# Three Strassen blocks in place of two, the first begun with four weight slices in the plain way

## The chip, the cores and the metric

One core of one Trainium2 chip runs the program. Its engines are TensorE (PE, matmul; PEld its weight loads), VectorE (DVE), ScalarE (ACT), GpSimd (POOL) and SyncE (SP, which here issues nearly all DMAs). They work side by side, each in the order of its own program, and wait for each other by semaphores. The metric is the time of one execution on the device in microseconds; lower is better. The kernel before takes 587.42 us in the median of three runs (587.04 to 587.86).

## The reference

Windowed attention over 4 x 8 heads, then a two-layer network over all 3072 tokens:

```python
for c in range(nc):                       # chunks of 32 queries
    k_full = concat([mem_k, k[l_start:r_end]])      # 8 memory keys, 16 left, 32 own, 8 right
    scores = scale * q_c @ k_full.T
    a = exp(scores - max); a = a / (sum(a) + 1e-09)
    out[c] = a @ v_full
x = out as (3072 tokens, 512)
h = x @ w_in                              # 512 x 2048
g = maximum(h, 0) + alpha * minimum(h, 0)
y = g @ w_out                             # 2048 x 512
```

All is fp32. A product of two fp32 numbers is made on PE as three products of a high and a low part (low x high, high x low, high x high): each operand is split into a rounded part and what is left of it. So every matrix of weights or tokens needs a split (a cast and a subtraction), and every product is three matmuls.

## The kernel before

**Tiles.** The tokens are eight halves of 384. A unit is one half and one pair of heads (32 units; units 4i to 4i + 3 make half i). `w_in` and `w_out` lie on chip as 16 slices f of 128 hidden features; slice f of both has one place in SBUF (`wps[f]`). A *slice* of a half costs 4 x 3 = 12 matmuls of 384 columns up (L764, `h_ps`), a bend (ACT `below` L773, DVE `bend` L776), a split of the result (ACT `high` L782, DVE `low` L786), and 3 x 3 = 9 matmuls of 512 columns down (L794, `o_ps`).

**The plain part.** Halves 0 to 3 (`NPLAIN = 4`) are made slice by slice. `ORDER` lists these 64 *places*: halves 0 and 1 side by side for the first slices, while the weights arrive and are decoded (ACT and DVE, L674 to L703; slice f is needed at the place of (0, f), so all 16 by place 24), then half 1's rest, then halves 2 and 3. The down products of a place run on PE after the up products of the next one.

**Attention.** Units 0 to 7 are made first, in another way. From place 20 on, pairs of units follow at the places in `BEGIN`: scores on PE (L344), maximum on DVE (L367), exponentials on ACT (L378), scaling on POOL (L399), 28 transposes on DVE (L420), and later the values on PE (L445). `split` leaves the result as a high and a low part for a plain half, `copy_raw` as it is for a Strassen half.

**The Strassen part.** Two blocks of 768 tokens (`NBIG = 2`, `big(s)`): two halves of tokens by two slices of weights make a 2 x 2 product with 7 products (6 matmuls each, L1089, `b_ps`) instead of 8. A *pair* i is two slices. The tokens are turned into seven forms (B11, B21, B22 as they are, T1 to T4 sums; POOL L951, split by ACT L937 and DVE or POOL L941), which lie in the places of weight slices no longer needed (`wps[2]` to `wps[8]`). The sums of weights are made once: `put_far(i, place)` (POOL L874, L877, L884; ACT L881; 12 POOL instructions for each of 8 pairs) is started at place `FIRST_SUM = 26` and every `SUM_EVERY = 3` places, and writes them to HBM; `load(f)` brings them back pair by pair into `wps[9]` to `wps[15]`. Each of the seven products goes into the four results by adds (DVE L1109). The first half's slices are bent, split and sent down with the next pair; the second half's wait (`gs`, `plain`) and go down after the last pair (L1059).

**What sets the order.** `Plan` holds every step with its engine, a cost that the author wrote, what it reads and writes, and how much work should still lie behind it (`rest`). `send` puts the steps out by a list schedule over these costs. On each engine the order is then fixed. The `gate` of a place is written by its up products, and `put_far` waits for that of the place before its own.

Of the kernel before, what the change touches and what calls it, by code (L numbers as in the profile page):

```python
# [37 lines left out]
NPLAIN = 4  # L38
# [58 lines left out]
STARTS_LONG = [x + 1 for x in BEGIN if FIRST_LONG - 1 <= x < len(ORDER)] + [len(ORDER)]  # L97

FORMS = ("T2", "B11", "B21", "T1", "T3", "B22", "T4")
FIRST_SUM, SUM_EVERY = 26, 3  # L100
# [3 lines left out]
FIRST_FRONT = 12  # L104
# [82 lines left out]
def body(ctx: ExitStack, tc: tile.TileContext, qvw, kw, whole, heads, w_in, w_out, alpha, out):  # L187
# [312 lines left out]
    def raw_at(k, half):  # L500

        if half == 0 and k < 2:
            return (k, 0, None), ("tmp", k)
        return spot(k, half % 2, 2)

    def plain_at(at_):

        if at_ not in plain:
            k, hl, blk = at_
            if blk is None:  # L510
                plain[at_] = tmp.tile([P, BT], F32, name="plain", tag=f"o{k}")
# [223 lines left out]
    def hidden(blk, f, first_f, last_f):  # L735

        joint = blk == 1 and f < NJOINT
        place = PLACE[blk, f]
        hk, sd, gh, gl = (x + str(place % n)
# [44 lines left out]
        def low():  # L784
            h["gl"] = room("gl", gl)
            nc.vector.tensor_tensor(out=h["gl"], in0=h["g"], in1=h["gh"].bitcast(F32), op=ALU.subtract)  # L786
# [20 lines left out]
        def add_bend():  # L807
# [3 lines left out]
            step(DVE, 0.56, low, reads=[sd, gh], writes=[gl] + new)  # L811
# [27 lines left out]
    def store(blk, o_ps):  # L839
# [12 lines left out]
        for tt in range(NTT):  # L852
            at_ = (None, None, [("tmp", tt)]) if blk == 1 else leave_at(blk == NPLAIN - 1)
# [74 lines left out]
    def forms(s):  # L928
        slow = ("B11", "B21")

        def split(name, ap, key, p):
            x = FORMS.index(name)

            def high():
                if p == 0:
                    xf[x] = wps[2 + x, 0].tile([P, 2, 2, BT], F32R, name="xf", tag="w")
                nc.scalar.copy(out=xf[x][:, 0, p], in_=plain_at(ap))  # L937

            def low():
                eng = nc.gpsimd if name in slow else nc.vector  # L940
                eng.tensor_tensor(out=xf[x][:, 1, p], in0=plain_at(ap), in1=xf[x][:, 0, p].bitcast(F32), op=ALU.subtract)  # L941

            claim = slot_keys(2 + x) + [("slot", x)] + [("X", x, hl, n) for hl in range(2) for n in range(2)]
            step(ACT, 0.53, high, reads=[key] + ([("slot", x)] if p else []), writes=[("X", x, 0, p)] if p else claim)
            step(*((POOL, 1.05) if name in slow else (DVE, 0.57)), low, reads=[key, ("slot", x), ("X", x, 0, p)], writes=[("X", x, 1, p)])

        for p in range(2):
            (b11, b12), (b21, b22) = [[raw_at(k, 2 * s + h) for h in range(2)] for k in (p, p + 2)]

            def less(to, a, b):  # L950
                step(POOL, 0.95, lambda: nc.gpsimd.tensor_tensor(out=plain_at(to[0]), in0=plain_at(a[0]), in1=plain_at(b[0]), op=ALU.subtract),  # L951
                     reads=[a[1], b[1]], writes=[to[1]])

            split("B11", *b11, p)
            split("B21", *b21, p)
# [29 lines left out]
    def load(f):  # L985
# [19 lines left out]
    def big(s):  # L1005
        ups, downs = UP[s % 2], UP[1 - s % 2]
        half = NPLAIN + 2 * s
        o = [{}, {}]

# [40 lines left out]
        def chunk(which, f, tt, last=NF - 1):  # L1050
            bank = (downs, ups)[which][tt]
            h = g[which, f]

            def go():
                if f == 0:
                    o[which][tt] = bank_of(bank)
                w = wa[s, which, f // 2]
                for i, (gk, wk) in enumerate((("gl", 0), ("gh", 1), ("gh", 0))):
# [3 lines left out]
                        rhs=w[:, f % 2, wk].bitcast(F32R),  # L1062
                        start=(f == 0 and i == 0), stop=(f == NF - 1 and i == 2),
                    )

            pe(0.69, go, [("wa", home[s, which, f // 2]), f"gh{f % 4}", f"gl{f % 4}"], [bank[2]])

        def used(which, i):
            load(home[s, which, i])

        def pair(i):
            n = s * NFP + i
# [3 lines left out]
            def w(x, at_):  # L1076
                return lambda wk, p: wa[n, x][:, at_ + wk * HALF + p * P:at_ + wk * HALF + (p + 1) * P]

            def wide(at_):
                return lambda wk, p: wa[n, 0][:, at_ + wk * 2 * HALF + p * P:at_ + wk * 2 * HALF + (p + 1) * P]  # L1080

            def product(bank, x, weight, name):
# [13 lines left out]
                pe(1.05, go, [("wa", home[n, x])] + [("X", xi, hl, p) for hl in range(2) for p in range(2)], [bank[2]])  # L1096
# [65 lines left out]
            for x in range(2):  # L1162
                load(home[n, x])
# [29 lines left out]
        def meet(olds, news):  # L1193
            attend(0, olds, news, at_=len(ORDER) + clock[0] / PAIR)
            clock[0] += 1.2 + (1.1 if news else 0)
            for u in olds:
                split(u, bank(u)[2])
                if u + 2 < NU:
                    load_v(u + 2)
            for u in news:  # L1200
                unit_begins(u)

        if s == 0:
            for f in queues:
                load(f)
        forms(s)
        news = []
        for i in range(NFP):
            for u in news:
# [177 lines left out]
```

## Time and profile before

| what | value |
|---|---|
| median of 3 runs | 587.42 us (587.04 to 587.86) |
| the profiled execution's own time | 587.05 us |
| its span, first to last instruction | 585.2 us |
| granted clock of PE | 1.00 in every stretch |
| first scores of the second kind (place 20) | 107.88 us |
| begin of POOL's weight sums | 121.2 us |
| begin of the first Strassen block's products | 322.1 us |
| begin of the second one's | 457.0 us |

Times in the profile are microseconds from the first instruction. In a group of instructions stand its line, engine, operation, `out<-in` and count, then its busy time and the mean length of one in ns, then the idle time of the engine just before them and what ended it. Lengths of one engine's instructions may overlap by some 0.05 to 0.1 us, as the next one starts before the last has written all.

### The profile page before, as it was taken

How to read it: one execution, taken by the hardware profiler on the slowest of the kernel's cores; microseconds unless marked ns; L12 is line 12 of the kernel's file. 1: busy time of each engine (PE TensorE's matmuls, PEld its weight loads, DVE VectorE, ACT ScalarE, POOL GpSimd, SP SyncE). 2: the span in 40 equal slices, each digit the busy share in tenths (PEclk: the TensorE clock that was granted, in tenths of full speed). 3: DMA queues.
4: the chain of work that ended last, by engine and by line, in shares of the span. 5: the costliest groups of instructions: out<-in, count | busy, mean ns of one | idle time of the engine just before them, and what ended most of it. 6: DMA issues, size and time to landing. Idle time of an engine off the chain costs nothing.

```text
span 585.2 us, 11938 instructions
## 1 busy us (share of the span) xinstructions
PE 575.6 (98%) x4503; PEld 511.4 (87%) x4503; DVE 435.6 (74%) x965; ACT 294.1 (50%) x774; POOL 145.4 (25%) x194
## 2 busy tenths in 40 slices
PE   7999999999999999999999999999999999999997
PEld 4899999889988989889988999999888999999886
DVE  7979999885948678687598896887959766656420
ACT  3888888725534536546437336336454432323421
POOL 5640000050876383723115000003014100000000
PEclk9999999999999999999999999999999999999999
DMA  8999300226767868551366977777796856776921
GB/s 316 402 416 416 128 0 2 67 66 227 294 231 285 304 204 344 175 192 37 103 200 219 347 255 267 268 286 297 287 297 227 274 231 244 251 285 229 317 92 54
DMA packets 40648, 133.70 MB, mean 228 GB/s; under 512 B 4624, under 2 KB 10000, under 8 KB 34448
## 3 DMA queue, kind: packets, MB, share of 16 engines
q1 hardware_dynamic: 40448, 132.82, 62.9%
q8 instruction: 35, 0.57, 0.4%
q14 instruction: 21, 0.17, 0.1%
q10 hardware_dynamic: 144, 0.13, 0.1%
HBM read 103.57 MB, written 29.36 MB: 227 GB/s over the span
## 4 chain that ended last, share of the span: by engine, by line
PE 87%; POOL 6%; DMA 3%; DVE 2%; issue 1%; ACT 1%; SPq 1%; POOLq 0%
PE b_ps L1059 23%; PE b_ps L1089 20%; PE o_ps L794 18%; PE h_ps L764 18%; PE a_ps L445 3%; PE s_ps L344 2%; POOL sum L874 2%; POOL form L884 2%; POOL sum L877 2%; PE a_ps L610 1%; DMA early<-heads 1%; DMA far_b<-w 1%; PE o_ps L597 1%; DMA qk<-kw 1%; DVE xf L941 1%
## 5 line engine op out<-in xcount | busy, mean ns | idle before, releaser
L764 PE MATMUL h_ps<-xh,w 128*128 128x384 f32 x512 | 130.5, 335 | 0.0
L1089 PE MATMUL b_ps<-xf,wa 128*128 128x384 f32 x672 | 125.3, 335 | 0.1
L1089 PEld LDWEIGHTS b_ps<-xf,wa 128*128 128x128 f32 x672 | 118.1, 188 | 4.8 <-DVE u L1109 0.4
L420 DVE STREAM_TRANSPOSE pt<-e 32x192 f32<-32x192 f32 (+1 forms) x336 | 100.0, 301 | 11.8 <-POOL e L399 6.1
L764 PEld LDWEIGHTS h_ps<-xh,w 128*128 128x128 f32 x512 | 92.7, 188 | 1.1
L764 PE MATMUL h_ps<-xl,w 128*128 128x384 f32 x256 | 87.8, 343 | 0.7 <-DVE g L776 0.6
L794 PE MATMUL o_ps<-w,xh 128*128 128x512 f32 x264 | 82.3, 393 | 0.0
L1109 DVE TENSOR_TENSOR u<-b_ps,u 128x384 f32<-128x384 f32 x112 | 60.2, 554 | 29.5 <-PE b_ps L1089 25.9
L399 POOL TENSOR_TENSOR e<-e,den 128x384 f32<-128x384 f32 x24 | 21.5, 900 | 243.2 <-DVE den L396 123.6
L1024 ACT ACTIVATE g<-u 128x384 f32<-128x384 f32 x64 | 33.5, 525 | 81.7 <-DVE u L1109 77.9
L1059 PE MATMUL b_ps<-wo,xh 128*128 128x512 f32 x192 | 59.8, 393 | 0.0
L1059 PE MATMUL b_ps<-wo,gh 128*128 128x512 f32 x192 | 59.6, 392 | 0.0
L794 PEld LDWEIGHTS o_ps<-w,xh 128*128 128x128 f32 x264 | 49.5, 188 | 9.8
L794 PE MATMUL o_ps<-w,xl 128*128 128x512 f32 x132 | 51.8, 393 | 0.2 <-DVE xl L786 0.2
L764 PEld LDWEIGHTS h_ps<-xl,w 128*128 128x128 f32 x256 | 48.1, 188 | 4.2 <-DVE g L776 1.0
L773 ACT ACTIVATE g<-h_ps 128x384 f32<-128x384 f32 x64 | 31.5, 492 | 40.2 <-PE h_ps L764 38.9
L776 DVE SCALAR_TENSOR_TENSOR g<-g,rise,h_ps 128x384 f32<-128x384 f32 x64 | 39.1, 611 | 16.2 <-ACT g L773 15.2
L378 ACT ACTIVATE e<-s_ps,mx 128x64 f32<-128x64 f32 x144 | 43.3, 318 | 9.9 <-DVE mx L370 9.8
L1059 PEld LDWEIGHTS b_ps<-wo,gh 128*128 128x128 f32 x192 | 36.0, 188 | 6.9
L1059 PEld LDWEIGHTS b_ps<-wo,xh 128*128 128x128 f32 x192 | 36.0, 188 | 6.7
L1059 PE MATMUL b_ps<-wo,xl 128*128 128x512 f32 x96 | 37.6, 391 | 0.0
L1059 PE MATMUL b_ps<-wo,gl 128*128 128x512 f32 x96 | 37.5, 390 | 0.0
(98 smaller groups left out, 874.2 us busy)
## 6 DMA issues: line engine op xcount, KB each, us to landing
wo<-far_o SPq DMA_DIRECT2D x32, 1024.0 KB, 5.1
wa<-far_a SPq DMA_DIRECT2D x16, 1024.0 KB, 4.8
wa<-far_b SPq DMA_DIRECT2D x16, 768.0 KB, 6.2
w_t<-w_in SPq DMA_DIRECT2D x16, 512.0 KB, 9.8
w_t<-w_out SPq DMA_DIRECT2D x16, 512.0 KB, 9.5
far_o<-w SPq DMA_DIRECT2D x16, 512.0 KB, 6.4
qk<-kw SPq DMA_DIRECT2D x24, 272.0 KB, 4.8
v_t<-qvw SPq DMA_DIRECT2D x24, 256.0 KB, 4.9
```

The source lines that it names most:

```text
L378: nc.scalar.activation(out=st["e"][:, i], in_=st["s"][h2][:, n], func=AF.Exp, scale=SCALE, bias=d["mx"][:, u - us[0], n, h2:h2 + 1], accum ...
L399: nc.gpsimd.tensor_tensor(out=st["e"], in0=st["e"], in1=st["den"].broadcast_to([P, NJ * 2, KW]), op=ALU.mult)
L420: nc.vector.transpose(out=pts[u % NPT][quad * CH:(quad + 1) * CH, j, t0:t0 + n1 - n0].rearrange("p t h q -> p (t h) q"), in_=(st["e"], zer ...
L445: nc.tensor.matmul(out=st["a"][h2 * D:(h2 + 1) * D, t * TQ:(t + 1) * TQ], lhsT=st["v"][:, t, h2, :], rhs=pts[u % NPT][:, :, t, h2, :], sta ...
L764: nc.tensor.matmul(out=h["ps"][:, :BT], lhsT=ws[f, 0][:, wk, k * P:(k + 1) * P], rhs=parts(blk, k)[1](xk), start=(k == 0 and n == 0), stop ...
L773: nc.scalar.activation(out=h["g"], in_=h["ps"][:, :BT], func=AF.Relu, scale=-1.0)
L776: nc.vector.scalar_tensor_tensor(out=h["g"], in0=h["g"], scalar=rise[:, f:f + 1], in1=h["ps"][:, :BT], op0=ALU.mult, op1=ALU.add)
L794: nc.tensor.matmul(out=o_ps[tt], lhsT=h[gk][:, tt * P:(tt + 1) * P], rhs=ws[f, 1][:, wk], start=(f == first_f and i == 0), stop=(f == last ...
L1024: nc.scalar.activation(out=h[name], in_=src(), func=AF.Relu, scale=-1.0)
L1059: nc.tensor.matmul(out=o[which][tt], lhsT=h[gk][:, tt * P:(tt + 1) * P], rhs=w[:, f % 2, wk].bitcast(F32R), start=(f == 0 and i == 0), sto ...
L1089: nc.tensor.matmul(out=h[bank[1]][:, :BT], lhsT=weight(wk, p).bitcast(F32R), rhs=xf[xi][:, xk, p], start=p == 0 and k == 0, stop=p == 1 an ...
L1109: nc.vector.tensor_tensor(out=h[t], in0=h[bank[1]][:, :BT], in1=h[t if of is None else of], op=ALU.add)
```

## The change

`NPLAIN` goes from 4 to 2, so that `NBIG` becomes 3: `ORDER` has 32 places, halves 2 and 3 join the Strassen part. Since all weight sums must be in HBM earlier, `put_far` starts at place 9 and not at 26. The first Strassen block does slices 12 to 15 (`BEFORE`) in the plain way, from the weights still on chip, with the tokens' forms B11 and B21 (first half) and then B12 and B22 (second half, a new form that shares its place with T4); the other six pairs are Strassen's. So this block begins before units 14 and 15 have their values. From place 20 on the subtraction `low` goes to POOL, as do those of T3 and T4. The scores and values of units 16 to 31 now fall into blocks 0 and 1, at `AT_PAIR` and `AT_REST`.

```diff
-NPLAIN = 4
+NPLAIN = 2
...
-PAIR, BIG = 4.7, 288.0
-BEGIN = (20, 26, 31, 36, 41, 46, 51, 55, 59, 71.3, 79.1, 86.5)
-AT_PAIR = {3: 26, 6: 28}
-AT_REST = {2: 30, 11: 32}
+PAIR, BIG = 4.7, 438.4
+BEGIN = (20, 24, 28, 32, 36, 40.3, 48.2, 55.8, 59.8, 69.4, 77.3, 85)
+AT_PAIR = ({2: 18, 5: 20}, {3: 26, 6: 28}, {})
+AT_REST = ({2: 22, 11: 24}, {2: 30, 11: 32}, {})
+BEFORE = (12, 13, 14, 15)
...
-FORMS = ("T2", "B11", "B21", "T1", "T3", "B22", "T4")
-FIRST_SUM, SUM_EVERY = 26, 3
+FORMS = ("T2", "B11", "B21", "T1", "T3", "B22", "T4", "B12")
+FIRST_SUM, SUM_EVERY = 9, 3
+FIRST_SLOW = 20
...
+        slow = place >= FIRST_SLOW
...
-            nc.vector.tensor_tensor(out=h["gl"], in0=h["g"], in1=h["gh"].bitcast(F32), op=ALU.subtract)
+            (nc.gpsimd if slow else nc.vector).tensor_tensor(out=h["gl"], in0=h["g"], in1=h["gh"].bitcast(F32), op=ALU.subtract)
...
-            step(DVE, 0.56, low, reads=[sd, gh], writes=[gl] + new)
+            step(*((POOL, 1.05) if slow else (DVE, 0.56)), low, reads=[sd, gh], writes=[gl] + new)
...
-        slow = ("B11", "B21")
+        slow = ("B11", "B21", "T3", "T4")
...
+    pairs_of = [list(range(NFP - len(BEFORE) // 2 if b == 0 else NFP)) for b in range(NBIG)]
...
+        def plain_up(f, which, n):
+            bank = ups[n % 2]
+            names = (("B11", "B21"), ("B12", "B22"))[which]
+            h = {}
+            g[which, f] = {}
+            def go():
+                h["ps"] = bank_of(bank)[:, :BT]
+                for k in range(NK):
+                    for m, (wk, xk) in enumerate(((0, 1), (1, 0), (0, 0))):
+                        nc.tensor.matmul(
+                            out=h["ps"],
+                            lhsT=ws[f, 0][:, wk, k * P:(k + 1) * P],
+                            rhs=xf[FORMS.index(names[k // 2])][:, xk, k % 2],
+                            start=(k == 0 and m == 0), stop=(k == NK - 1 and m == 2),
+                        )
+            pe(2.1, go, [("w", 0, f, 0), ("w", 0, f, 1)] + [
+                ("X", FORMS.index(x), hl, p) for x in names for hl in range(2) for p in range(2)], [bank[2]])
+            if which:
+                bent(h, "g", lambda: h["ps"], bank[2], f, *kept_at(f))
+            else:
+                sk = bent(h, "g", lambda: h["ps"], bank[2], f)
+                rooms(g[which, f], "g", f, lambda: h["g"], sk)
...
         if s == 0:
-            for f in queues:
+            for p in range(2):
+                (b11, b12), (b21, b22) = raws(p)
+                split_form("B11", *b11, p)
+                split_form("B21", *b21, p)
+            for f in (9, 10, 11):
                 load(f)
-        forms(s)
+            meet(14, None)
+            for n, f in enumerate(BEFORE):
+                plain_up(f, 0, n)
+            think()
+            for f in BEFORE[:2]:
+                whole(0, f)
+            meet(16, None)
+            for f in BEFORE[2:]:
+                whole(0, f)
+            for p in range(2):
+                (b11, b12), (b21, b22) = raws(p)
+                split_form("B12", *b12, p)
+                split_form("B22", *b22, p)
+            for n, f in enumerate(reversed(BEFORE)):
+                plain_up(f, 1, n)
+            for f in range(12, NF):
+                load(f)
+        forms(s > 0)
+        for i in pairs:
+            think()
+            if i in AT_PAIR[s]:
+                meet(AT_PAIR[s][i], ups)
+            pair(i)
```

Here `meet(u, ...)` makes the values of units u - 2 and u - 1 and the scores of u and u + 1; `whole(0, f)` sends a slice of the first half down (L1071 in the new kernel), from the weights on chip for the slices of `BEFORE`.

Three places of the built order, before and now (the new kernel's lines are shifted by a few: `low` is L782 there, the weight sums are L870, L873 and L880). First POOL, after it has cleared the transposed tiles (L635, L638 before; L630, L633 now). Before:

```order
L638 MEMSET pt_977 128x768
L399 TENSOR_TENSOR e<-e,den 128x384 x2
L874 TENSOR_TENSOR sum<-w 128x256 x2
L877 TENSOR_TENSOR sum<-sum 128x256
L874 TENSOR_TENSOR sum<-w 128x256
L877 TENSOR_TENSOR sum<-sum 128x256 x2
```

and now:

```order
L633 MEMSET pt_977 128x768
L870 TENSOR_TENSOR sum<-w 128x256 x2
L873 TENSOR_TENSOR sum<-sum 128x256
L870 TENSOR_TENSOR sum<-w 128x256
L873 TENSOR_TENSOR sum<-sum 128x256 x2
L870 TENSOR_TENSOR sum<-w 128x256
L873 TENSOR_TENSOR sum<-sum 128x256
L880 TENSOR_TENSOR form<-sum,form 128x256 x4
```

The sums stood behind the first two scalings of the attention; now those of four pairs and the first five instructions of the fifth stand ahead of the first scaling (L399), in the time of the decoding.

Second, DVE in that time, at about place 14. In both kernels the names are the same and the lines differ by four or five: the decoding's gather (L682 before, L677 now), end (L686, L681), join (L690, L685) and subtraction (L703, L698), the bend (L776, L772) and the low (L786, L782). Before:

```order
L776 SCALAR_TENSOR_TENSOR g<-g,rise,h_ps 128x384
L690 SCALAR_TENSOR_TENSOR a<-a,w_t 128x1024
L682 COPY w_t<-w_t 128x512
L686 TENSOR_SCALAR w_t<-w_t 128x1024
L786 TENSOR_TENSOR xl<-g,xh 128x384
L703 TENSOR_TENSOR w<-a,w 128x2x512
L776 SCALAR_TENSOR_TENSOR g<-g,rise,h_ps 128x384
L690 SCALAR_TENSOR_TENSOR a<-a,w_t 128x1024
L786 TENSOR_TENSOR xl<-g,xh 128x384
L682 COPY w_t<-w_t 128x512
L686 TENSOR_SCALAR w_t<-w_t 128x1024
```

and now:

```order
L698 TENSOR_TENSOR w<-a,w 128x2x512
L772 SCALAR_TENSOR_TENSOR g<-g,rise,h_ps 128x384
L685 SCALAR_TENSOR_TENSOR a<-a,w_t 128x1024
L677 COPY w_t<-w_t 128x512
L782 TENSOR_TENSOR xl<-g,xh 128x384
L698 TENSOR_TENSOR w<-a,w 128x2x512
L772 SCALAR_TENSOR_TENSOR g<-g,rise,h_ps 128x384
L681 TENSOR_SCALAR w_t<-w_t 128x1024
L685 SCALAR_TENSOR_TENSOR a<-a,w_t 128x1024
L782 TENSOR_TENSOR xl<-g,xh 128x384
```

Next to nothing moved on DVE: a gather and an end have changed places with the bend and the low beside them. What is new is that POOL has the sums above to do at the same time.

Third, PE where the plain part ends (`a_ps` are values, of units 12 and 13 in the first piece of the new kernel and of 14 and 15 in the second; `s_ps` the scores; `b_ps` the Strassen part's products, whose tokens' forms are `xf`). Before, the block's pairs follow the last down products:

```order
L794 MATMUL o_ps<-w,gh 128x512 x2
L794 MATMUL o_ps<-w,gl 128x512
L794 MATMUL o_ps<-w,gh 128x512 x2
L1089 MATMUL b_ps<-xf,wa 128x384 x42
L344 MATMUL s_ps<-qk_189 32x64 x24
L344 MATMUL s_ps<-qk_190 32x64 x24
L1089 MATMUL b_ps<-xf,wa 128x384 x18
```

and now:

```order
L790 MATMUL o_ps<-w,gl 128x512
L790 MATMUL o_ps<-w,gh 128x512 x2
L445 MATMUL a_ps<-pt_975,v_t 64x96 x8
L445 MATMUL a_ps<-pt_977,v_t 64x96 x8
L1107 MATMUL b_ps<-xf,w 128x384 x48
L1071 MATMUL b_ps<-w,xl 128x512
L1071 MATMUL b_ps<-w,xh 128x512 x2
```

and, after these first down products from `xl` and `xh` (L1071):

```order
L1071 MATMUL b_ps<-w,xh 128x512 x2
L346 MATMUL s_ps<-qk_189 32x64 x24
L346 MATMUL s_ps<-qk_190 32x64 x24
L445 MATMUL a_ps<-pt_975,v_t 64x96 x8
L445 MATMUL a_ps<-pt_977,v_t 64x96 x8
L1071 MATMUL b_ps<-w,gl 128x512
L1071 MATMUL b_ps<-w,gh 128x512 x2
L1071 MATMUL b_ps<-w,gl 128x512
```

and after those, the second half's plain slices and the first pair:

```order
L1071 MATMUL b_ps<-w,gh 128x512 x2
L1107 MATMUL b_ps<-xf,w 128x384 x48
L1139 MATMUL b_ps<-xf,wa 128x384 x42
L346 MATMUL s_ps<-qk_189 32x64 x24
L346 MATMUL s_ps<-qk_190 32x64 x24
L1139 MATMUL b_ps<-xf,wa 128x384 x18
```

The values of units 12 to 15, which were made beside the plain part of halves 2 and 3, now stand between plain slices of the first Strassen block; the first pair (L1139) comes after 96 plain up products (L1107) and 36 down products (L1071), and not at once.

More of the change, by code (lines that the diff above doesn't have):

```diff
@@ L926, in body @@
     xf = {}
-    def forms(s):
-        slow = ("B11", "B21")
[L931 to L945, printed above, removed]
-        for p in range(2):
[L948 to L955, printed above, removed]
@@ new lines, in split_form, with high, low @@
+    def split_form(name, ap, key, p):
+        x = FORMS.index(name)
+        f = 2 + min(x, FORMS.index("T4"))
+        def high():
+            if p == 0:
+                xf[x] = wps[f, 0].tile([P, 2, 2, BT], F32R, name="xf", tag="w")
+            nc.scalar.copy(out=xf[x][:, 0, p], in_=plain_at(ap))
+        def low():
+            eng = nc.gpsimd if name in slow else nc.vector
+            eng.tensor_tensor(out=xf[x][:, 1, p], in0=plain_at(ap), in1=xf[x][:, 0, p].bitcast(F32), op=ALU.subtract)
+        slow = ("B11", "B21", "T3", "T4")
+        same = [y for y in range(len(FORMS)) if 2 + min(y, FORMS.index("T4")) == f]
+        claim = slot_keys(f) + [("slot", f)] + [("X", y, hl, n) for y in same for hl in range(2) for n in range(2)]
+        step(ACT, 0.53, high, reads=[key] + ([("slot", f)] if p else []), writes=[("X", x, 0, p)] if p else claim)
+        step(*((POOL, 1.05) if name in slow else (DVE, 0.57)), low, reads=[key, ("slot", f), ("X", x, 0, p)], writes=[("X", x, 1, p)])
@@ new lines, in raws, with forms, less @@
+    def raws(p):
+        return [[spot(k, h, 2) for h in range(2)] for k in (p, p + 2)]
+    def forms(plain_too=True):
+        def less(to, a, b):
+            step(POOL, 0.95, lambda: nc.gpsimd.tensor_tensor(out=plain_at(to[0]), in0=plain_at(a[0]), in1=plain_at(b[0]), op=ALU.subtract),
+                 reads=[a[1], b[1]], writes=[to[1]])
+        for p in range(2):
+            (b11, b12), (b21, b22) = raws(p)
+            if plain_too:
+                split_form("B11", *b11, p)
+                split_form("B21", *b21, p)
@@ L1008, in big @@
         o = [{}, {}]
+        pairs = pairs_of[s]
+        turns = [list(BEFORE) if s == 0 else [], list(range(NF))]
+        turns[0] = turns[0] + [f for f in range(NF) if f not in turns[0]]
         def pe(cost, fn, reads, writes):
@@ L1068, in used, with kept_at, place @@
+            pe(0.69, go, ([("w", 1, f, 0), ("w", 1, f, 1)] if own else [("wa", home["o", s, which, f // 2])]) + [
+                f"gh{f % 4}", f"gl{f % 4}"], [bank[2]])
         def used(which, i):
-            load(home[s, which, i])
+            load(home["o", s, which, i])
+        def kept_at(f):
+            to, key = keep_place(f)
+            if to is not None:
+                return (lambda: plain_at(to)), [key]
+            i = f // 2
+            def place():
+                if (s, i) not in gs:
+                    gs[s, i] = wps[i // 2, i % 2].tile([P, 2, BT], F32, name="gs", tag="w")
+                return gs[s, i][:, f % 2]
+            return place, [("gs", 2 * i), ("gs", 2 * i + 1)] + [("w", i % 2, i // 2, hl) for hl in range(2)] if f % 2 else [key]
@@ L1226, in big @@
         used(1, 0)
-        for f in (NF - 2, NF - 1):
+        think()
+        for f in (2 * pairs[-1], 2 * pairs[-1] + 1):
             whole(0, f)
-        used(0, NFP - 1)
+        used(0, pairs[-1])
         leave(0, range(NTT))
-        last = s == NBIG - 1
         for f in range(2, NF - NEND if last else NF):
-            if news and s == 0 and f == min(AT_REST) + 1:
-                for u in news:
-                    weights(u)
-                    turn(u)
-                news = []
+            think()
             take(f)
```

138 lines of the change are left out of this document (64 added, 74 removed).

## The prediction

> **What bounds the kernel now.** I read the busy shares first, then the waits, then the chain that ended last, then single stretches.
>
> ```profile
> span 585.2 us, 11938 instructions
> PE 575.6 (98%) x4503; PEld 511.4 (87%) x4503; DVE 435.6 (74%) x965; ACT 294.1 (50%) x774; POOL 145.4 (25%) x194
> DVE  7979999885948678687598896887959766656420
> POOL 5640000050876383723115000003014100000000
> GB/s 316 402 416 416 128 0 2 67 66 227 294 231 285 304 204 344 175 192 37 103 200 219 347 255 267 268 286 297 287 297 227 274 231 244 251 285 229 317 92 54
> ```
>
> A busy PE is only a hint, so the waits of PE come next (columns: who waited for whom, us in total, times, longest).
>
> ```profile
> PE o_ps L794 <- DVE gl L786: 0.7, 1, 0.7
> PE h_ps L764 <- DVE g L776: 0.6, 1, 0.6
> PE h_ps L764 <- DVE xl L486: 0.2, 1, 0.2
> PE o_ps L794 <- DVE xl L786: 0.2, 1, 0.2
> ```
>
> After the start-up PE waits 1.7 us in all. So the kernel's time is the sum of PE's instructions at their spacing. The chain in order of time (start, us) gives that spacing:
>
> ```profile
> 57.67 2.10 PE h_ps L764 x12
> 59.78 2.08 PE o_ps L794 x9
> 119.71 1.17 PE s_ps L344 x82
> 139.74 1.47 PE a_ps L445 x32
> 335.31 2.08 PE b_ps L1089 x12
> 448.62 8.38 PE b_ps L1059 x36
> ```
>
> A 384-wide matmul takes 2.08/12 = 0.173 us, a 512-wide one 8.38/36 = 0.233 at most, a group of scores 1.17, of values 1.47.
>
> **The sum is made against the profiled execution**, 587.05 us, of which 585.2 are span; the 1.85 around it stay. It lies 0.37 below the median of the runs, 587.42, inside their spread (587.04 to 587.86).
>
> **Removed on PE.** For 768 tokens the plain way makes 16 slices x 12 matmuls x 2 halves = 384 wide-384 products; pairs make 8 x 42 = 336. With four slices (two pairs) left plain it is 6 x 42 + 4 x 2 x 12 = 348: 36 fewer. The 512-wide products, the score groups and the value groups are as many as before. 36 x 0.173 = **-6.24 us**.
>
> **Moved: the weight sums.** The 96 POOL instructions of the eight far pairs began at 121 us; now the first pair is released by place 8, whose up products end at 57.67 + 2.10 = 59.8. Four pairs, 48 instructions, now lie before the first scores (place 20, 107.9 us), on top of the weight decoding. There the stretch 59.8 to 107.9 (windows; busy us and count of PE, PEld, DVE, ACT, POOL) shows no POOL at all and hardly any idle DVE:
>
> ```profile
> 59.80:72.30 12.50, 12.50 (x64) 11.32 (x64) 11.96 (x16) 10.39 (x13) 0.00 (x0) 1.00 0.28 108
> 97.50:107.90 10.40, 10.40 (x61) 9.03 (x67) 9.90 (x12) 6.63 (x11) 0.00 (x0) 1.00 0.00 1
> sum 48.10, PE 48.10 PEld 43.18 DVE 44.72 ACT 38.21 POOL 0.00; mean PE 12.03 PEld 10.79 DVE 11.18 ACT 9.55 POOL 0.00
> ```
>
> DVE is idle 48.10 - 44.72 = 3.38 us. Its order there (L776 bend, decode steps, L786 low) is fixed, and the low decides when PE may go down. Two of these lows, by DVE's own timeline:
>
> ```profile
> 93.84 0.61 DVE L776 SCALAR_TENSOR_TENSOR g<-g,rise,h_ps 128x384 f32<-128x384 f32 x1
> 94.37 1.22 DVE L690 SCALAR_TENSOR_TENSOR a<-a,w_t 128x1024 int32<-128x1024 int32 x1
> 96.97 0.55 DVE L786 TENSOR_TENSOR xl<-g,xh 128x384 fp32r<-128x384 f32 x1
> ```
>
> The low stands three decode steps behind its bend and ends at 97.52; PE has been through its 4.18 us of other work (2.10 + 2.08) by then, so there is next to no slack: what DVE loses, PE loses. The decode's lead of several slices doesn't help, since the low is queued behind it.
>
> And DVE does lose, when POOL runs. A low that started beside a POOL subtraction took three times its length and ended 0.4 us behind it; the other way round a POOL product beside a DVE subtraction took 1.65:
>
> ```profile
> 29.21 1.33 POOL L703 TENSOR_TENSOR w<-a,w 128x512 fp32r<-128x512 f32 x1 [1.78 <-ACT w L698]
> 29.31 1.64 DVE L786 TENSOR_TENSOR xl<-g,xh 128x384 fp32r<-128x384 f32 x1
> 119.41 1.18 DVE L703 TENSOR_TENSOR w<-a,w 128x1024 fp32r<-128x1024 f32 x1
> 119.63 1.65 POOL L399 TENSOR_TENSOR e<-e,den 128x384 f32<-128x384 f32 x1 [3.51 <-ACT xh L782]
> ```
>
> The instructions of the stretch that read two tiles of SBUF (L690, L703, L786) or run at two elements a cycle (L686, 1024 in 0.69 us), without POOL; and then the lows of 148 to 246 us beside POOL's sums (count, busy, mean ns):
>
> ```profile
> L690 DVE SCALAR_TENSOR_TENSOR a<-a,w_t 128x1024 int32<-128x1024 int32 x9 | 11.0, 1224 | 0.0
> L703 DVE TENSOR_TENSOR w<-a,w 128x1024 fp32r<-128x1024 f32 x8 | 9.8, 1221 | 0.1
> L686 DVE TENSOR_SCALAR w_t<-w_t 128x1024 int32<-128x1024 int32 x9 | 6.2, 694 | 0.6
> L786 DVE TENSOR_TENSOR xl<-g,xh 128x384 fp32r<-128x384 f32 x11 | 6.1, 557 | 1.7 <-ACT xh L782 1.6
> ...
> L786 DVE TENSOR_TENSOR gl<-g,gh 128x384 fp32r<-128x384 f32 x11 | 8.2, 749 | 1.8 <-ACT gh L782 1.7
> L786 DVE TENSOR_TENSOR xl<-g,xh 128x384 fp32r<-128x384 f32 x10 | 7.7, 769 | 1.2 <-ACT xh L782 1.0
> L877 POOL TENSOR_TENSOR sum<-sum 128x256 f32<-128x256 f32 x28 | 21.9, 782 | 1.0
> ```
>
> 37 such instructions (9 + 8 + 9 + 11) meet 48 POOL instructions of some 0.78. Bounds of one wait: below, 0.20 us, as the lows of 148 to 246 show (0.758 against 0.557), where such DVE instructions were rare; above, half a POOL instruction, 0.39, since here half of them follow one another directly and POOL gets its turn in between. I take 0.27, nearer to the row of the same instruction: 37 x 0.27 = 10.0 us, less the 3.38 of idle time that can swallow it: **+6.6 us** (ends: 37 x 0.20 - 3.4 = 4.0, and 37 x 0.39 - 3.4 = 11.0). Should DVE's waits fall only where the low isn't next, it is 0.
>
> The Trainium skill (SBUF — State Buffer, "SBUF: two separate sides") says that a VectorE instruction with two SBUF inputs or in a two-port mode and a GpSimd instruction hold one shared port pair in turn, each for its whole length, and the loser fully blocks. The two pairs of rows above agree (1.64 and 1.65 us). By it both engines' work of the stretch is one queue: 33.1 us of DVE and 48 x 0.78 = 37.4 of POOL, 70.5 in a stretch of 48.1, and the sum would carry up to +22 in the place of +6.6.
>
> ACT gets 16 form casts there (0.4 us each, 6.5) beside 38.21 of 48.10: it still fits.
>
> **Lows on POOL from place 20.** Twelve of them, and T3 and T4's, leave DVE for POOL:
>
> ```profile
> L941 POOL TENSOR_TENSOR xf<-plain,xf 128x384 fp32r<-128x384 f32 x8 | 8.1, 1042 | 3.7 <-ACT xf L937 2.0 <-PE b_ps L1089 1.7
> L399 POOL TENSOR_TENSOR e<-e,den 128x384 f32<-128x384 f32 x24 | 21.5, 900 | 243.2 <-DVE den L396 123.6 <-ACT e L378 74.0 <-DVE den L393 33.8
> L843 DVE TENSOR_TENSOR o_t<-o_ps,o_t 128x512 f32<-128x512 f32 x3 | 2.0, 691 | 3.8 <-PE o_ps L794 3.8
> L420 DVE STREAM_TRANSPOSE pt<-e 32x192 f32<-32x192 f32 x168 | 61.9, 369 | 9.1 <-POOL e L399 6.1
> L420 DVE STREAM_TRANSPOSE pt<-e 32x64 f32<-32x64 f32 x168 | 38.1, 234 | 2.6
> 448.63 7.47 POOL L951 TENSOR_TENSOR plain<-plain 128x384 f32<-128x384 f32 x6 [7.48 <-ACT plain L524]
> ```
>
> From place 20 to the value group of units 14 and 15, PE has 12 places x 4.18, the four plain slices and four groups each of scores and values, some 73 us; POOL has 48 x 0.78 + 8 x 0.9 + 16 x 1.04 + 2 x 1.25 = 64. Hidden, if POOL isn't late at its begin.
>
> **The junction.** Between the last down products of the plain blocks and the values of units 14 and 15 PE has 1.47 + 48 x 0.173 + 18 x 0.233 + 1.17 = 15.1 us; DVE's order puts three sums of L843, 28 transposes, three bends, two lows and small steps there: 2.1 + 8.4 + 1.8 + 1.1 + 0.4 = 13.8. It fits by 1.3 us. Then T2 is due 4.2 + 8.3 + 2.1 = 14.6 us after these values and needs four subtractions of 1.25 and a split: hidden. From one big block to the next, T4 now needs 7.47 + 4 x 1.04 = 11.6 us of POOL against 8.38 + 5 x 1.04 = 13.6 of PE: hidden, with 2 us left. The old waits, 1.7 us, all lie in products that are gone; for such narrow fits I put half of them back: **-0.85** (ends -1.7 and, with 3 us at the junction, +1.3).
>
> **Transfers.** A pair reads 1.75 MB and one of 1 MB in 42 x 0.173 + 18 x 0.233 = 11.5 us: 240 GB/s, as the slices of the big blocks now show (230 to 350) without a wait. Hidden. DVE's work changes by +42 adds, +32 bends and lows, less the plain ones: under 7 us of 150 idle.
>
> 587.05 - 6.24 + 6.6 - 0.85 = **586.6 us**; the likeliest case's own range, by the ends of the wait, is 584.0 to 591.
>
> **Rivals.** (1) DVE's waits stay within its idle time: PE alone decides, 587.05 - 6.24 - 0.85 = **580.0**. For it: before, DVE was at nine tenths in that stretch and PE never waited; against it: 7.4 us of waits at the least into 3.38. (2) The shared port decides, and the time is **slower**: the waits are 0.39 each and DVE's idle time is of no use, since its gaps are waits for ACT in short loops: 587.05 - 6.24 - 0.85 + 37 x 0.39 = **594.4**. It decides from 0.09 us a wait on (3.38/37) at the lows of places 9 to 20; POOL then falls behind too, and the first softmax scaling (L399), queued behind 53 of its sums, makes the values late. For it: the 1.64 and 1.65 us. Against it: POOL may idle between a sum and its form, waiting for ACT. The Trainium skill's rule above (SBUF — State Buffer, "SBUF: two separate sides") is this case, and its 22 us the worst of it. (3) The wait moves to the junction, DVE's 13.8 us running 3 us over while the early stretch loses only 2: 587.05 - 6.24 + 2 + 3 = **585.8**. (4) The change isn't what it says: the order of the built program has the 36 fewer products, so hardly.
>
> **Numbers.** Forecast 0.44, rivals 0.28, 0.21, 0.05, 0.02. A measurement of this kernel tells 0.2% (1.2 us) from no change: bounds 586.2 and 588.6. The forecast's range gives 0.14 faster, 0.18 same, 0.12 slower; (1) is faster, (2) slower, (3) 0.03 faster and 0.02 same, (4) same: faster 0.45, same 0.22, slower 0.33. The range for 8 in 10 reaches from rival 1 to just short of rival 2: 580.0 to 594.0.
>
> **What would show it.** Right: the first scores (place 20) start 4 to 11 us after 107.9; the decode subtractions and L690 take 1.4 to 1.6 us there and not 1.22; PE's waits name DVE's low at the down products. From there on PE's spacing is as before and 36 matmuls are missing. Wrong: those scores at 108 (rival 1), or PE waiting for the values' transposes or POOL's scaling (rival 2), or its first big wait at the junction (rival 3). The sum fails altogether if a transfer or a bank, which I cost at nothing, stops PE inside a pair.

## The result, and the profile after

The changed kernel takes 596.42 us in the median of four runs (595.18 to 596.54), beside 587.3 us of four runs of the kernel before (587.04 to 587.86): a ratio of 1.0149, 95% interval 1.0132 to 1.0167. It is slower by 9 us. The forecast was 586.6 with a range of 580.0 to 594.0; time and sign were wrong, and the rival that came nearest was the second, the shared port (594.4).

The profiled execution has a span of 594.7 us, 9.5 more than before. From its page:

```profile
span 594.7 us, 12044 instructions
PE 575.0 (97%) x4467; PEld 508.3 (85%) x4467; DVE 456.5 (77%) x987; ACT 302.2 (51%) x796; POOL 201.7 (34%) x230
POOL 5663395997699460001123500101212500000000
PEclk9999999897999999999999999999999999999999
```

and PE's waits (who waited for whom, us in total, times, longest):

```profile
PE h_ps L760 <- DVE g L772: 5.6, 1, 5.6
PE o_ps L790 <- DVE xl L782: 5.1, 2, 4.2
PE b_ps L1107 <- DVE plain L1035: 1.2, 1, 1.2
```

PE has the 36 matmuls less (4503 to 4467), as foretold, but its busy time is down by only 0.6 us, since a part of them ran slowly, and it waits where it never waited before. POOL's busy time went from 145.4 to 201.7 us, of which some 36 are new work (36 instructions more, of about 1.0 us); the other 20 are longer instructions. The windows, with busy us and count of PE, PEld, DVE, ACT, POOL, then the granted clock, show where:

```profile
84.90:97.50 12.60, 11.73 (x57) 9.49 (x56) 12.50 (x15) 9.02 (x12) 6.17 (x5) 1.00 0.53 209
97.50:116.00 18.50, 14.30 (x85) 12.13 (x92) 18.36 (x18) 11.98 (x20) 17.92 (x14) 0.91 0.44 171
116.00:135.00 19.00, 13.44 (x248) 12.15 (x234) 13.48 (x25) 9.46 (x37) 17.11 (x20) 0.96 0.83 290
135.00:150.00 15.00, 15.00 (x64) 13.03 (x64) 11.13 (x30) 6.63 (x27) 12.79 (x16) 0.82 0.38 147
```

DVE has next to no idle time left from 85 to 116 us, POOL little from 97 to 135, and PE's granted clock (the last column but two) is below full twice: it is 0.50 from 109.7 to 113.1 and from 133.6 to 140.4 us. The first scores of place 20 start at 115.83 us (before 107.88).

**What the sums cost DVE and POOL.** Groups of DVE and POOL, first before (41 to 110 us), then after (41 to 118 us, the same work): busy us, mean ns.

```profile
L690 DVE SCALAR_TENSOR_TENSOR a<-a,w_t 128x1024 int32<-128x1024 int32 x12 | 14.7, 1223 | 0.0
L703 DVE TENSOR_TENSOR w<-a,w 128x1024 fp32r<-128x1024 f32 x11 | 13.4, 1221 | 0.2 <-ACT w L698 0.2
L786 DVE TENSOR_TENSOR xl<-g,xh 128x384 fp32r<-128x384 f32 x17 | 9.5, 557 | 1.7 <-ACT xh L782 1.6
L686 DVE TENSOR_SCALAR w_t<-w_t 128x1024 int32<-128x1024 int32 x13 | 9.0, 694 | 1.4 <-ACT w_t L682 0.5
L682 DVE COPY w_t<-w_t 128x512 int16<-128x512 int16 x11 | 8.4, 762 | 0.0
```

```profile
L698 DVE TENSOR_TENSOR w<-a,w 128x1024 fp32r<-128x1024 f32 x11 | 16.7, 1518 | 0.0
L685 DVE SCALAR_TENSOR_TENSOR a<-a,w_t 128x1024 int32<-128x1024 int32 x12 | 16.2, 1351 | 0.1
L782 DVE TENSOR_TENSOR xl<-g,xh 128x384 fp32r<-128x384 f32 x17 | 13.9, 816 | 0.1
L677 DVE COPY w_t<-w_t 128x512 int16<-128x512 int16 x11 | 11.1, 1008 | 0.0
L681 DVE TENSOR_SCALAR w_t<-w_t 128x1024 int32<-128x1024 int32 x12 | 10.5, 872 | 0.9 <-ACT w_t L677 0.5
L772 DVE SCALAR_TENSOR_TENSOR g<-g,rise,h_ps 128x384 f32<-128x384 f32 x16 | 9.7, 605 | 0.0
...
L870 POOL TENSOR_TENSOR sum<-w 128x256 f32<-128x256 f32 x15 | 18.1, 1219 | 0.2
L873 POOL TENSOR_TENSOR sum<-sum 128x256 f32<-128x256 f32 x15 | 18.1, 1205 | 1.0
L880 POOL TENSOR_TENSOR form<-sum,form 128x256 fp32r<-128x256 f32 x12 | 15.4, 1305 | 24.8 <-ACT form L877 24.8
```

DVE lost 11 x 0.297 + 12 x 0.128 + 17 x 0.259 + 11 x 0.246 + 12 x 0.178 = 14.1 us. Two wider gathers, not shown, lost another 0.8. Of these groups only the bend (L772), with one of its inputs in PSUM, kept its 0.61. POOL's 42 sums lasted 51.6 us, 1.23 each, against 0.74 where nothing was beside them: it lost 42 x 0.49 = 20.6 us, more than DVE.

Of the 8.0 us by which the first scores are late, 5.1 are PE's waits for the low (L782). Behind the longer of them, 4.2 us, the clock is at half, and the 9 down products there take 3.56 us in place of 2.08: another 1.5. The other 1.4 are spread over smaller delays.

**The second wait.** The chain of waits in order of time (start, us):

```profile
128.59 0.72 POOL sum L873
...
129.39 0.72 POOL sum L870
130.11 0.80 POOL e L401
...
130.93 0.37 DVE pt L422
...
133.79 0.62 DVE g L772
...
134.46 4.21 PE h_ps L760 x12
138.67 4.98 PE o_ps L790 x18
```

POOL is behind with its sums, so the first scaling (L401) is late; DVE stands at the first transpose (L422), with the bend (L772) queued behind it; and PE waits for the bend. Then 12 up products take 4.21 us in place of the 2.28 that they took behind the same scores before, and 18 down products 4.98 in place of 4.12: 2.8 us lost to the half clock.

So, from the profiled execution of before: 587.05 - 6.24 (the products) - 1.7 (the old waits, gone) + 8.0 (first scores) + 5.6 (the bend) + 2.8 (the clock behind it) + 1.2 (the junction, L1107) = 596.7. The profiled execution took 596.48; 0.2 is not accounted for.

### The profile page after: what moved, and what is told of

Same layout as the page of the kernel before. It is cut to its first block, busy times and chain, and to the rows that moved or that the text cites. A ratio compares the mean times of both kernels' runs of the same rounds, so it can differ in the third digit from the quotient of the medians.

```text
span 594.7 us, 12044 instructions
## 1 busy us (share of the span) xinstructions
PE 575.0 (97%) x4467; PEld 508.3 (85%) x4467; DVE 456.5 (77%) x987; ACT 302.2 (51%) x796; POOL 201.7 (34%) x230
## 4 chain that ended last, share of the span: by engine, by line
PE 75%; POOL 5%; DVE 4%; issue 1%; ACT 1%; POOLq 0%; ACTq 0%
PE b_ps L1071 33%; PE b_ps L1139 27%; PE o_ps L790 4%; PE h_ps L760 4%; PE a_ps L445 3%; PE b_ps L1107 2%; PE s_ps L346 2%; POOL form L880 2%; POOL sum L870 2%; POOL sum L873 1%; DVE xf L935 1%; DVE w L698 1%; DVE w_t L677 0%; DVE a L685 0%; DVE pt L422 0%
## 5 line engine op out<-in xcount | busy, mean ns | idle before, releaser
L1139 PE MATMUL b_ps<-xf,wa 128*128 128x384 f32 x924 | 172.7, 336 | 0.1
L1139 PEld LDWEIGHTS b_ps<-xf,wa 128*128 128x128 f32 x924 | 161.9, 188 | 7.0 <-ACT plain L519 0.7
L422 DVE STREAM_TRANSPOSE pt<-e 32x64 f32<-32x64 f32 (+1 forms) x336 | 99.5, 301 | 14.8 <-POOL e L401 9.1
L1071 PE MATMUL b_ps<-wo,xh 128*128 128x512 f32 x276 | 86.0, 393 | 0.0
L1071 PE MATMUL b_ps<-wo,gh 128*128 128x512 f32 x276 | 85.6, 392 | 0.0
L401 POOL TENSOR_TENSOR e<-e,den 128x384 f32<-128x384 f32 x24 | 20.4, 850 | 141.3 <-DVE den L398 137.1
L760 PE MATMUL h_ps<-xh,w 128*128 128x384 f32 x256 | 66.9, 343 | 0.0
L1071 PEld LDWEIGHTS b_ps<-wo,gh 128*128 128x128 f32 x276 | 51.8, 188 | 9.9
L1071 PEld LDWEIGHTS b_ps<-wo,xh 128*128 128x128 f32 x276 | 51.8, 188 | 9.7
L790 PE MATMUL o_ps<-w,xh 128*128 128x512 f32 x168 | 53.9, 403 | 0.0
L1071 PE MATMUL b_ps<-wo,gl 128*128 128x512 f32 x138 | 53.9, 390 | 0.0
L1071 PE MATMUL b_ps<-wo,xl 128*128 128x512 f32 x138 | 53.9, 390 | 0.0
L760 PE MATMUL h_ps<-xl,w 128*128 128x384 f32 x128 | 45.1, 352 | 5.6 <-DVE g L772 5.6
L760 PEld LDWEIGHTS h_ps<-xh,w 128*128 128x128 f32 x256 | 47.4, 192 | 1.3 <-DVE w L698 0.6
L949 POOL TENSOR_TENSOR plain<-plain 128x384 f32<-128x384 f32 x24 | 26.7, 1137 | 46.0 <-ACT plain L519 45.4
L880 POOL TENSOR_TENSOR form<-sum,form 128x256 fp32r<-128x256 f32 x32 | 32.1, 1026 | 29.0 <-ACT form L877 29.0
L1035 DVE SCALAR_TENSOR_TENSOR g<-g,rise,u 128x384 f32<-128x384 f32 x44 | 28.2, 641 | 10.8 <-ACT g L1032 10.3
```

The costliest lines, as they stand in the source:

```text
L401: nc.gpsimd.tensor_tensor(out=st["e"], in0=st["e"], in1=st["den"].broadcast_to([P, NJ * 2, KW]), op=ALU.mult)
L422: nc.vector.transpose(out=pts[u % NPT][quad * CH:(quad + 1) * CH, j, t0:t0 + n1 - n0].rearrange("p t h q -> p (t h) q"), in_=(st["e"], zer ...
L760: nc.tensor.matmul(out=h["ps"][:, :BT], lhsT=ws[f, 0][:, wk, k * P:(k + 1) * P], rhs=parts(blk, k)[1](xk), start=(k == 0 and n == 0), stop ...
L790: nc.tensor.matmul(out=o_ps[tt], lhsT=h[gk][:, tt * P:(tt + 1) * P], rhs=ws[f, 1][:, wk], start=(f == first_f and i == 0), stop=(f == last ...
L880: nc.gpsimd.tensor_tensor(out=t["s", x][:, 1], in0=t[n], in1=t["s", x][:, 0].bitcast(F32), op=ALU.subtract)
L1035: nc.vector.scalar_tensor_tensor(out=to() if to else h[name], in0=h[name], scalar=rise[:, f:f + 1], in1=src(), op0=ALU.mult, op1=ALU.add)
```

## The experiments

Theory, once the traces were compared: POOL's sums beside the decoding make both engines wait, and POOL's lateness then makes the bend late. Rivals: the loss belongs to the new order of the blocks; to the transfers and casts that come with the sums; or to POOL's queue alone, whatever DVE does. One run each, beside runs of the kernel before on the same chip at 587.18 to 587.44 us. "Scores" is the start of the first scores of place 20.

| run | us | scores at | PE's longest waits after 30 us |
|---|---|---|---|
| kernel before | 587.3 | 107.9 | none over 0.7 |
| changed kernel | 596.42 | 115.8 | bend 5.6, low 4.2 |
| early_sums | 601.62 | 116.6 | bend 5.0, low 4.2 |
| small_sums | 580.69 | 108.5 | junction 1.1 |
| memset_sums | 580.05 | 107.9 | junction 1.2 |
| dear_sums | 591.85 | 111.4 | bend 2.0, L1071 1.7 |
| late_sums | 601.10 | 108.4 | bend 5.5, POOL's low 4.1 |
| spread_sums | 600.45 | 108.6 | transfers 4.3 and 3.0 |
| fill_wait | 593.79 | 117.2 | low 4.2, bend 1.2 |
| lows_dve | 600.06 | 116.8 | low 4.2, bend 4.0 |
| dve_three | 595.31 | 110.1 | transposes 4.2, L1072 3.3 |
| dve_one | 593.50 | 108.0 | L1072 2.5, transfer 2.2 |

L1071, in the last two L1072, is the down product of the Strassen part; it waits there for a low of DVE.

**early_sums: the early sums alone, in the kernel before.**

```diff
-FIRST_SUM, SUM_EVERY = 26, 3
+FIRST_SUM, SUM_EVERY = 9, 3
```

> The kernel before with one part of the change alone: the weight sums begin at place 9 and not at 26; all else (two Strassen blocks, lows on DVE) is the old kernel. If POOL's sums beside the decoding make the loss (port), the first scores of place 20 come at 114 to 117 us in place of 107.9, DVE's two-input instructions last 0.3 to 0.5 us longer there, and the time is 595 to 603 us. If the loss belongs to the new order of the blocks or to the junction, the time stays at 587 to 589 us.

601.62 us, 14.4 more than the kernel before, with two Strassen blocks and nothing else changed. PE's waits are those of the changed kernel:

```profile
PE h_ps L764 <- DVE g L776: 5.6, 2, 5.0
PE o_ps L794 <- DVE xl L786: 5.0, 2, 4.2
```

The rival of the blocks' order falls: 601.6 less the 6.24 us of the products is 595.4, and the changed kernel takes 596.4.

**small_sums: the changed kernel without POOL's load.**

```diff
-            nc.gpsimd.tensor_tensor(out=t[n], in0=w(f, 0, k2).bitcast(F32), ...)
+            nc.gpsimd.tensor_tensor(out=t[n][:, :8], in0=w(f, 0, k2)[:, :8].bitcast(F32), ...)
```

(and so for the sums of sums and the lows; the tiles are cleared once and kept)

> The changed kernel with POOL's 96 weight sums cut to 8 of 256 columns (so the sums' values are wrong; the same instructions in the same order, the same casts on ACT and the same transfers). If the port and POOL's lateness make the loss, the first scores come at 108 to 109 us, PE has no wait over 0.5 us up to 200 us and never runs at half its clock after 30 us, and the time is 579.5 to 583 us (the sum without any wait said 580.0; the junction's 1.3 us may stay). If the transfers or ACT's casts make it, or the order itself, the time stays above 590.

580.69 us; the first rival's sum without any wait was 580.0. The transfers and ACT's casts are all still there, so they cost nothing here, and the Strassen part does give its 6.2 us. The gather (L677) still takes 1.02 us and not 0.76, beside sums of 8 columns; its 11 instructions lose 2.8 us, but the first scores come only 0.6 us late. The only wait left is the junction's, 1.1 us, and DVE's timeline shows what stands ahead of the bend there:

```profile
188.55 3.62 DVE L947 TENSOR_TENSOR xf<-plain,xf 128x384 fp32r<-128x384 f32 x3 [0.25 <-ACT xf L943]
```

It looks like one more case of the same kind: three lows of DVE take 3.62 us, 1.2 each and not 0.56, while POOL makes the tokens' sums. That is read from the trace; no run took it apart.

**memset_sums: a POOL as busy, which doesn't read SBUF.**

```diff
-            nc.gpsimd.tensor_tensor(out=t[n], in0=t[a], in1=t[b], op=op)
+            clear(t[n])
```

(and so for the other two kinds of sum; `clear` makes two memsets of its tile)

> The changed kernel with each of POOL's 96 weight sums replaced by two memsets of the same 256 columns (no sums are made; POOL writes SBUF and doesn't read it). A memset of 768 columns takes 0.75 us, so the pair some 0.5 to 0.7. If it is the reading of SBUF by both engines that makes them wait for each other, DVE's instructions of the decoding keep their lengths (L698 1.24, L685 1.22, L782 0.56), the first scores come at 108 to 110, and only POOL's queue stays: 580.5 to 585 us. If any busy POOL holds DVE up, the first scores come at 113 to 116 and the time is 590 to 597.

580.05 us, just under the first answer's 580.5, and the lengths between 41 and 118 us say why:

```profile
L685 DVE SCALAR_TENSOR_TENSOR a<-a,w_t 128x1024 int32<-128x1024 int32 x13 | 15.8, 1219 | 0.1
L698 DVE TENSOR_TENSOR w<-a,w 128x1024 fp32r<-128x1024 f32 x12 | 14.7, 1222 | 0.2
...
L782 DVE TENSOR_TENSOR xl<-g,xh 128x384 fp32r<-128x384 f32 x18 | 10.0, 554 | 1.1 <-ACT xh L778 0.9
L681 DVE TENSOR_SCALAR w_t<-w_t 128x1024 int32<-128x1024 int32 x13 | 9.4, 726 | 1.1 <-ACT w_t L677 0.7
L677 DVE COPY w_t<-w_t 128x512 int16<-128x512 int16 x11 | 9.0, 816 | 0.0
...
L867 POOL MEMSET sum<- 128x256 f32 x40 | 17.0, 425 | 2.3
L866 POOL MEMSET sum<- 128x256 f32 x40 | 14.7, 366 | 29.7 <-ACT form L881 29.5
```

Two memsets last 0.79 us, as long as a sum by itself. DVE's instructions with two inputs in SBUF have their lengths of before within 4 ns; those with one input (L681, L677) are a little longer (0.726 for 0.694, 0.816 for 0.762). So what holds up a DVE instruction that reads two tiles of SBUF is not a busy POOL, but one that reads SBUF at the same time. The Trainium skill (SBUF — State Buffer, "SBUF: two separate sides") says just this, that two SBUF inputs of DVE collide only with a GpSimd instruction that reads SBUF; here the runs agree. What holds up the instructions with one input, which lose far more beside the sums (0.872 and 1.008), was not taken apart.

**dear_sums: the plan is told that a sum costs 1.2.**

```diff
-step(POOL, 0.7, partial(full, n, f, k2), ...)
+step(POOL, 1.2, partial(full, n, f, k2), ...)
```

> The changed kernel, with 1.2 in place of 0.7 as the cost that the plan believes of a weight sum; the work is the same. 47 sums stand ahead of the first scaling of the softmax in place of 54. If the second wait of PE (5.8 us for the bend, and 3 us at half clock behind it) comes from POOL's queue ahead of the scaling, it falls to about 3 us and the half clock behind it goes: 589 to 592 us, with the first scores still at 115 to 116. If the port alone makes both waits, the time stays within 2 us of 596.4.

591.85 us; the second wait is 2.0 and nothing runs at half clock behind it, as expected. (The clock is at half once, from 198.3 to 201.7 us.) The first scores came at 111.4 and not 115 to 116: with other places for the sums (36 of them started ahead of the scores, not 40) the low waited 1.3 us at most in place of 4.2. That part was not foreseen. It is the best of the kernels that do the whole work with three Strassen blocks, and still 0.8% behind the kernel before.

**late_sums, spread_sums: the sums later.**

```diff
-FIRST_SUM, SUM_EVERY = 9, 3
+FIRST_SUM, SUM_EVERY = 18, 1
```

This is the edit of late_sums; spread_sums sets other places and another planned cost, which its expectation names.

> The changed kernel with the weight sums begun at place 18 and then at every place, so behind most of the decoding. If the port beside the decoding makes the loss, the first scores come at 107.5 to 109.5 us. POOL then has 96 sums, 16 lows, 8 scalings and 16 forms between 105 and some 215 us, so the forms or the loads of the first Strassen block come late by 0 to 10 us: 581 to 591 us in all. If the loss belongs to the order of the blocks, the time stays at 594 to 598 us.

> The changed kernel with the weight sums begun at places 14, 18, 22, 24, 26, 28, 30 and 31, and 1.0 in place of 0.7 as the cost that the plan believes. Fewer sums lie beside the decoding and the plan leaves room ahead of the scalings. If port and queue together are the loss, both waits shrink: first scores at 109 to 112, no wait of PE over 3.4 us, 584 to 591 us. If POOL's lateness only moves on to the junction (as with the sums begun at place 18), it stays at 592 to 600.

Both have the first scores back at 108.4 and 108.6: the decoding is undisturbed. Both lose it again: 601.1 us is worse than late_sums' 581 to 591, and 600.45 just over the second answer of spread_sums. PE's waits, late_sums first:

```profile
PE h_ps L760 <- DVE g L772: 5.9, 2, 5.5
PE o_ps L790 <- POOL xl L782: 4.1, 1, 4.1
```

```profile
PE b_ps L1071 <- DMA wo<-far_o: 6.3, 2, 4.3
PE b_ps L1139 <- DMA wa<-far_b: 3.0, 1, 3.0
```

With the sums at places 18 to 25 POOL is behind at places 20 to 30, where the scaling and, since this change, the lows are its own. With the sums spread to place 31 the last one ends at 234 us (changed kernel: 199), and the weights come back too late for the first Strassen block.

**fill_wait: matmuls for nobody in PE's second wait.**

```diff
             for u in news:
                 head_products(u)
+            if place == 24:
+                stir(ps_a.tile([P, DM], F32, name="fill", tag="a"), 13)
```

> The changed kernel with 13 matmuls of 512 bf16 columns, whose result nobody reads, behind the scores of place 24: they fill some 2.9 us of the 5.8 us in which PE waits for the bend. If PE's half clock after that wait comes from the wait's length, the 18 matmuls of 384 and 512 columns behind it run at 0.17 and 0.23 us in place of 0.32 and 0.43, and the time falls by about 3 us: 592.5 to 594. If something else makes them slow (port, banks, weight loads), the time stays at 596 to 597.

593.79 us. The bend comes at the same time, but PE goes on at full speed (PE's timeline):

```profile
130.42 2.75 PE L305 MATMUL fill<-busy 128*128 128x512 bf16 x12 [0.16 <-issue]
134.41 0.44 PE L762 MATMUL h_ps<-xl,w 128*128 128x384 f32 x1 [1.24 <-DVE g L774]
134.69 0.51 PE L762 MATMUL h_ps<-xh,w 128*128 128x384 f32 x2
```

The up products start at 134.41 as in the changed kernel at 134.46, and are 0.17 us apart, not 0.32. So the loss behind the wait is the clock's, and the clock fell for the wait: between 133.6 and 140.4 us it is 0.50 in the changed kernel and 1.00 here. The first scores come 1.4 us later than in the changed kernel, since the half clock behind the low's wait lasts 6.8 us and not 3.4, in a part that is the same in both. The Trainium skill (TensorE: Matmul & The Clock Gate, "Part 1: The HAM clock gate") gives about 3.4 us of idleness for the fall and as much work for the return. The falls agree in the changed kernel (waits of 4.2 and 5.6 us); its work behind them was slow for 3.0 and 5.9 us, the second longer than the Trainium skill's figure. In dear_sums the clock fell with no wait near that length: at 198.3 us, behind waits of 0.5 and 1.7 us, when PE had been busy for 1.44 of the 3.40 us before.

**lows_dve: the lows of places 20 to 31 back on DVE.**

```diff
-FIRST_SLOW = 20
+FIRST_SLOW = 99
```

> The changed kernel with one part undone: the lows of places 20 to 31 are DVE's again, as before the change. If POOL's queue is what is late, taking 12 subtractions of 1.0 us from it shortens the second wait by 1 to 3 us, and DVE, which is not the late engine there, hides them: 592 to 596 us. If the lows on POOL are a relief for a DVE that is itself the bound from place 20 on, it is 598 to 602.

600.06 us: the second answer. The bend's wait did shrink (4.0 for 5.6), but DVE then was late with the transposes' and the junction's work. Lows on POOL were worth 3.6 us in this one run, late POOL or not.

**dve_three, dve_one: DVE makes sums itself.**

```diff
-            nc.gpsimd.tensor_tensor(out=t[n], in0=t[a], in1=t[b], op=op)
+            (nc.vector if i in MERGE_DVE else nc.gpsimd).tensor_tensor(out=t[n], in0=t[a], in1=t[b], op=op)
```

(and so for the other two kinds of sum; the pairs i are 1, 2 and 3 in dve_three and 0 in dve_one)

> The changed kernel with the 36 weight sums of the pairs 1 to 3 made by DVE and not by POOL (same places, same work). Beside a POOL sum DVE lost 14.8 us for 42 sums, 0.35 each; making such a sum itself should cost it about 0.37 (a low of 384 columns takes 0.56). If the loss is waiting for POOL, DVE is no worse off and POOL is free: first scores at 108 to 112, no wait over 2 us for the bend behind the scores of place 24, and 587 to 592 us with what waits are left at the junction. If DVE's own work is the bound, whatever POOL does, the first scores come at 116 or later and the time is 597 or more.

> The same with the 12 sums of the first pair alone on DVE, so that POOL's first sum comes later. If what POOL does beside the decoding is the loss, the first scores come at 108 to 111 us and the time is 588 to 594; if POOL's later sums then fall behind their loads, PE waits for a transfer at 200 to 240 us, as it does with the sums spread out.

The first half of both expectations held: scores at 110.1 and 108.0, and no bend waited over 0.4 us. The time of dve_three did not follow (595.31, over its 592); that of dve_one did (593.5), with the transfer's wait, 2.2 us, that its expectation named. A sum of 256 columns takes DVE 0.44 us:

```profile
L874 DVE TENSOR_TENSOR sum<-sum 128x256 f32<-128x256 f32 x4 | 1.8, 442 | 0.0
L871 DVE TENSOR_TENSOR sum<-w 128x256 f32<-128x256 f32 x4 | 1.8, 439 | 0.0
```

What DVE spends on them it lacks later. In dve_three PE waits at the junction, and its clock is at half from 193.0 to 206.7 us:

```profile
PE a_ps L446 <- DVE pt L423: 4.4, 2, 4.2
PE b_ps L1072 <- DVE gl L1052: 3.3, 1, 3.3
```

No version with three blocks came below 591.85. Early on POOL, late on POOL, or on DVE: each place for the 96 sums that was tried cost 11 to 20 us against the 580.7 without them, and the blocks give 6.2.

## Why the prediction was wrong, step by step

- **36 products fewer, -6.24.** Right: small_sums and memset_sums come out at 580.7 and 580.1, rival 1's 580.0.
- **The weight sums, +6.6.** The first scores come 8.0 us later, inside the step's 4.0 to 11.0, but its working was off in three places. The step said that the first pair "is released by place 8, whose up products end at" 59.8: the first sum starts at 41.41 us. That gate orders the plan's list; on the chip POOL starts as soon as its queue and the weights allow. It counted 37 instructions of DVE and left out the gather (L677) in the belief that only two inputs in SBUF or the doubled rate count; it went from 0.76 to 1.01. And the wait of one is 0.13 to 0.30, not 0.27 throughout. The errors offset each other: DVE lost 14.1 us from 41 us on where 10.0 was said from 59.8 on, and more idle time lay in the longer stretch. And 1.5 of the 8.0 us is the half clock, for which the step had no term. That it came out so near is luck.

```profile
41.41 1.86 POOL L870 TENSOR_TENSOR sum<-w 128x256 f32<-128x256 f32 x2
```

- **"Hidden, if POOL isn't late at its begin."** This is the step that failed. It priced POOL's sums at 0.78, the row of 148 to 246 us, in a stretch where DVE was said to collide with them; only DVE's side was given a wait, though the prediction shows a POOL product of 1.65 us beside a subtraction of DVE. POOL's side is the larger: 1.23 for each of 42, some 20 us. POOL was late at its begin, and the 5.6 us for the bend and 2.8 us at half clock are what that cost: 8.4 us that the sum put at nothing. early_sums and small_sums show the cause, dear_sums and fill_wait the two parts.
- **The junction, "fits by 1.3 us".** It misses by 1.2 in the changed kernel and by 1.1 and 1.2 in the two without sums. The step took the lows there at 0.56; in the traces they last 1.2 beside POOL's sums of the tokens. With the old waits gone (-1.7) the term of -0.85 came out as -0.5, inside its ends.
- **T2, T4, the transfers, ACT's casts.** Hidden, as said: small_sums has them all. (The transfers stop being hidden once the sums come later, as in spread_sums.)
- **The rivals.** The second named the mechanism and its direction, slower, and said that the first scaling behind 53 sums would come late. It priced it by DVE's waits alone (594.4) and had "the values" late, not the bend behind the transposes. Its condition held ("from 0.09 us a wait on"). It was given a chance of 0.21, less than rival 1 with 0.28, since DVE's idle time was set against DVE's loss, and nothing was set against POOL's.
- **The forecast's own signs.** First scores 4 to 11 us after 107.9 held, and so did PE's wait for the low. Of the two lengths foreseen as 1.4 to 1.6, the decode subtraction took 1.52 and the join 1.35. "From there on PE's spacing is as before" is what failed.
- **The Trainium skill's rule** (SBUF — State Buffer, "SBUF: two separate sides"), with the worst case of 22 us that the prediction worked out from it: the sums cost 596.4 - 580.7 = 15.7 us. It was nearer to that whole loss than the 6.6 that the rows of a sparse stretch gave; but both were worked out for the stretch up to the first scores, and that one lost 8.0.

## What to carry to other kernels

Where two engines hold each other up, price both sides: here the engine with idle time to spare lost more (20.6 us beside 14.1), and whatever is queued behind it in order (here a scaling, then transposes, then the bend on which the bound engine waits) is late by that. Wait lengths read where such meetings were rare did not hold where both queues were full; there, add both engines' busy times and compare the sum with the stretch. And moving work to an earlier stage is free only if that stage has room on all the engines it meets; removing 36 matmuls was worth about their length (6.5 us in small_sums for 6.24), but only in a kernel without the load of the sums.

## What the runs showed of the hardware that was not expected

- A DVE instruction with two inputs in SBUF was not held up at all by POOL's memsets (1.222, 1.219 and 0.554 us beside them), and by 0.13 to 0.30 us in the mean by POOL's sums.
- A very short DVE instruction can wait for several times its length: 128 x 6 elements (L395, 0.17 without a neighbour) took 0.70 beside a sum, ahead of the softmax's scaling (L401), for which the transposes then wait 3.68 us:

```profile
126.33 0.70 DVE L395 TENSOR_SCALAR den<-den 128x6 f32<-128x6 f32 x1
...
130.93 1.51 DVE L422 STREAM_TRANSPOSE pt<-e 32x192 f32<-32x192 f32 x4 [3.68 <-POOL e L401]
```

- A long wait of PE cost more than its length: behind the 5.6 us for the bend the half clock cost another 2.8, and 13 matmuls without purpose took 2.7 of it back (594.7 to 592.0 in the span). Several short waits can do the same: in dear_sums PE was busy for 1.44 of 3.40 us, and the 3.40 us behind that ran at half clock.
